# Sliding-window attention and a top-1 mixture of experts: the gate's products on the whole TensorE array, V in two transfers, the first expert's weights split, and a new order

## The chip, the core and the time that is measured

One core of a Trainium2 chip runs the program. The profile calls its engines PE (TensorE; PEld is its weight load), DVE (VectorE), ACT (ScalarE), POOL (GpSimd) and SP (SyncE, which here only issues transfers). The metric is the device time of one execution, in microseconds (us).

## What is computed

Four batches of 768 tokens go through attention with 8 heads of 64. A token attends to the 128 tokens up to itself and to the first four of its batch (the sinks). Each of the 3072 rows of 512 that come out is given to the expert, out of eight, whose gate logit is largest, and is scaled by two gate values.

```python
keep = is_sink | in_window
scores = np.where(keep, scale * np.matmul(q, k.transpose(0, 1, 3, 2)), -1000000000.0)
a = np.exp(scores - np.max(scores, axis=-1, keepdims=True))
x = np.matmul(a / (np.sum(a, axis=-1, keepdims=True) + 1e-09), v)   # then [3072, 512]
logits = x @ w_gate;  e_idx = np.argmax(logits, axis=1)
eom = 1.0 / (1.0 + np.exp(-(x @ w_output_gate)))
for e in range(E):
    mask = e_idx == e
    h = np.maximum(x[mask] @ w1[e], 0.0)          # 512 -> 1024
    out[mask] = gate_w[mask, None] * eom[mask, e, None] * (h @ w2[e])
```

## The kernel before

**Attention.** The work is cut into 16 pairs of heads, four to a batch; `pair(p)` writes one. Its steps on PE are the scores in three groups (L1256, from q and k), six turns of e into f (L1305), the turn of the packed sink weights (`skT`), the products with V in six parts (L1373, `av0` to `av5`), those with the sinks' V (L1396, `avs`), the gate (L1412) and the turns of the output for the store (L1445, `n0`, `n1`). Between them DVE masks the scores and takes the maxima (L1265 to L1272), ACT does the exponentials (L1277) and copies f out (L1308), POOL masks f into g (L384), SP sends the packed sinks to another buffer (L1346), ACT makes a small copy between two parts of `av` (L1387, `tick`) and copies the finished output from PSUM into `ot` (L1402), which the gate and the turns both read. DVE weighs the gate's logits (L1420, `lw`) and scales x (L1448), POOL adds the logits to the batch's (L1428, L1430; DVE in the last two pairs), and SP stores x to `xd` (L1455).

Scores, `av`, `avs` and the gate use 64 x 64 quadrants of the array, four products side by side; everything else uses all 128 x 128. All of attention and the gate is fp32, and each fp32 product shows as two records in the trace. A gate is 24 products with 16 moving columns, 48 records. PE thus changes between two modes, "four" and full; the planner charges 170 ns and 150 ns for a change.

**Routing.** After a batch's last pair, `gate_route` (L524 to L627) turns its logits into positions: DVE steps, one count on PE (L555, L557), then the positions from it (`pos`, `base`, L567, L568), a large compare (`ohrow`, L600), a sort on PE (L619). After batches 1 and 2, `rank_experts` (`u`, L661 and L662) and `early_table` choose two experts each whose tokens so far can be worked on before attention ends: the early slots 0 to 3, 256 tokens each. The other 13 slots (`SEQ`) follow once batch 3 is routed.

**Experts.** A slot gathers its tokens (POOL, L899), turns them (L964), multiplies by w1 (M1), takes relu into hh (ACT), multiplies by w2 (M2), scales (y, L979) and scatters (POOL, L982). Weights arrive as 512 KB transfers into four `raw` buffers. ACT casts each into a high part (L939), DVE subtracts that from raw to make the low part (L943), and a product is then three fp32r products, high by high, low by high, high by low (M1 at L1083, M2 at L1122). With `PLAIN = 1` slot 0 goes another way: its weights land directly in the tiles `wa0` to `wa3`, no casts, and its products are single fp32 ones (M1 at L1064: 32 products of 256 columns; M2 in L1122: 16 of 512). Its M1 may start only behind the last score and its M2 only behind the last pair's `av0`, and both are "soft": the planner puts other ready work of PE ahead of them within a time `SOFT`.

**Order.** No order is written by hand. `Plan.order()` walks all steps with their costs and picks for each engine what is ready and due first; due times are the table `AT` by kind of step, `PIN` by number of step, and `SLOT0` for the experts. Each engine then runs its list in order, so a step that waits holds up all that stand behind it on that engine. `behind=` and `paced` add orders between steps of different engines, `touch` is a small POOL write to a buffer ahead of its first transfer.

## Time and profile before

| | |
|---|---|
| time of three executions | 514.12, 514.47 (median), 519.23 us |
| the profiled execution | 515.66 us; the profile's span in it 514.0 us |
| busy in the span | PE 480.6 us (94%), DVE 326.8 (64%), ACT 281.6 (55%), POOL 159.3 (31%) |
| mean granted clock of PE | 0.99 of full speed |
| moved by DMA | 112.35 MB, 217 GB/s of HBM traffic over the span |
| the first gate starts, the last | 24.50 us, 195.72 us |

Where a row reads `x48`, 48 instructions are meant; `[0.17 <-issue]` at a row's end is idle time ahead of it and what ended it, and "issue" is time in which the engine waited for nothing that the profile shows. The granted clock 1.00 is 2.4 GHz and half of it 1.2 GHz. The chain is the work that ended last, followed back from the end, each step to what released it.

### The profile page before, as it was taken

The page shows a single profiled execution, that of the slowest core. Times are in us where ns is not written, and L with a number is a line of the kernel's source. Part 1 is how long each engine was busy: PE and PEld are TensorE (multiplying, and loading weights), DVE is VectorE, ACT ScalarE, POOL GpSimd, SP SyncE. Part 2 cuts the span into 40 slices and gives each one's busy share as a digit, 9 for nine tenths or more (in the row PEclk, how much of TensorE's full clock was granted, in tenths as well). Part 3 has the DMA queues.
Part 4 walks back from the last instruction along what each step waited for, and adds up shares of the span by engine and source line. Part 5 has one row for each costly group of instructions (what it writes and reads, how often), then busy time and mean ns, then how long its engine had stood idle before and what let it go on. Part 6 is the DMA issues. An engine that isn't in the chain of part 4 may idle for free.

```text
span 514.0 us, 14382 instructions
## 1 busy us (share of the span) xinstructions
PE 480.6 (94%) x5625; PEld 390.4 (76%) x5625; DVE 326.8 (64%) x702; ACT 281.6 (55%) x774; POOL 159.3 (31%) x284
## 2 busy tenths in 40 slices
PE   7899988979899979999999999999999999999993
PEld 3677867757678866688898988978975977986861
DVE  5575866888686667559998963237525688267710
ACT  3878885657597534454556334246525667257510
POOL 5536543647653530204082113022203210101011
PEclk9999999979999999999999999999999999999998
DMA  6674664536695293856498753819679978888930
GB/s 203 214 224 111 220 217 126 169 100 195 200 346 178 87 297 94 282 176 204 153 307 319 233 205 96 294 46 339 199 275 332 331 270 284 301 297 320 352 121 29
DMA packets 61295, 112.35 MB, mean 219 GB/s; under 512 B 8027, under 2 KB 27617, under 8 KB 61218
## 3 DMA queue, kind: packets, MB, share of 16 engines
q1 hardware_dynamic: 56578, 97.06, 56.8%
q0 software_dynamic: 4352, 13.87, 7.5%
q8 instruction: 47, 0.77, 0.6%
q10 hardware_dynamic: 288, 0.41, 0.3%
q14 instruction: 30, 0.25, 0.2%
HBM read 98.14 MB, written 13.31 MB: 217 GB/s over the span
## 4 chain that ended last, share of the span: by engine, by line
PE 62%; DVE 13%; DMA 8%; ACT 6%; issue 6%; POOL 1%; another core or an unknown queue 1%; SPq 1%; POOLq 0%; DVEq 0%; ACTq 0%
PE d L1122 21%; PE d L1083 15%; DMA raw<-in_w_dram 5%; PE d L1373 5%; PE d L1256 4%; PE d L1096 3%; PE d L1064 3%; PE tp L1305 2%; ACT e L1277 2%; DVE nmx L1272 2%; PE tp L964 2%; PE tp L1445 2%; DVE d L1270 2%; PE d L1412 2%; PE d L1030 1%
## 5 line engine op out<-in xcount | busy, mean ns | idle before, releaser
L1277 ACT ACTIVATE e<-d,nmx 128x132 f32<-128x132 f32 x192 | 68.8, 369 | 1.4
L982 POOL DMA_INDIRECT out_dram<-y,idx x20 | 21.2, 1058 | 136.8 <-ACT y L979 107.8
L1000 ACT ACTIVATE hh<-d 128x512 fp32r<-128x512 f32 (+1 forms) x32 | 20.7, 649 | 58.4 <-PE d L1083 56.6
L1256 PE MATMUL d<-k,q 64*64 64x196 f32 (+3 forms) x1088 | 44.2, 283 | 6.8 <-DVE lw L1420 2.0
L1256 PEld LDWEIGHTS d<-k,q 64*64 64x64 f32 x1088 | 36.8, 134 | 15.1 <-issue 6.1
L1003 DVE SCALAR_TENSOR_TENSOR hl<-d,hh 128x512 fp32r<-128x512 f32 (+1 forms) x32 | 24.0, 753 | 34.6 <-ACT hh L1000 34.3
L899 POOL DMA_INDIRECT xg<-xd,idx x20 | 24.5, 1224 | 67.3 <-PE tp L964 44.3
L1373 PE MATMUL d<-f,v 64*64 64x64 f32 (+1 forms) x768 | 41.3, 252 | 2.0 <-ACT e L1277 1.2
L1373 PE MATMUL d<-g,v 64*64 64x128 f32 (+1 forms) x640 | 38.9, 253 | 3.8 <-ACT tick L1387 2.3
L384 POOL TENSOR_SCALAR_AFFINE_SELECT g<-f 128x512 f32<-128x512 f32 (+1 forms) x48 | 27.7, 577 | 43.7 <-ACT f L1308 41.7
L1277 ACT ACTIVATION_READ_ACCUMULATOR e<-d,nmx 128x1 f32 x192 | 39.1, 203 | 0.0
L1373 PEld LDWEIGHTS d<-f,v 64*64 64x64 f32 x768 | 34.1, 135 | 5.9 <-issue 2.5
L1270 DVE COPY_PREDICATED d<-maskf,d 128x512 f32<-128x512 int32 (+1 forms) x48 | 29.0, 604 | 14.0 <-PE d L1256 8.9
L1272 DVE TENSOR_REDUCE nmx<-d 128x4 f32<-128x528 f32 x48 | 33.9, 707 | 1.7
L979 ACT ACTIVATE y<-d,sc 128x512 f32<-128x512 f32 (+1 forms) x28 | 17.5, 656 | 30.6 <-PE d L1122 21.4
L1373 PEld LDWEIGHTS d<-g,v 64*64 64x64 f32 x640 | 29.8, 134 | 5.6 <-ACT tick L1387 3.1
L1305 PE MATMUL tp<-ident,e 128*128 128x128 f32 x192 | 30.3, 285 | 2.4 <-DVE x L1448 1.3
L1308 ACT COPY f<-tp 128x512 f32<-128x512 f32 x48 | 27.5, 586 | 6.6 <-PE tp L1305 6.4
L1305 PEld LDWEIGHTS tp<-ident,e 128*128 128x128 f32 x192 | 21.3, 143 | 10.4 <-DVE x L1448 2.3
L384 POOL TENSOR_SCALAR_AFFINE_SELECT f<-f 128x512 f32<-128x512 f32 (+1 forms) x48 | 27.0, 563 | 3.3
L982 POOL DMA_INDIRECT out_dram<-y,idx_e x8 | 11.8, 1480 | 51.4 <-ACT y L979 49.9
L1284 ACT ACTIVATE nmx<-nmx 128x4 f32<-128x4 f32 x48 | 10.0, 209 | 26.9 <-DVE nmx L1272 26.6
(481 smaller groups left out, 1447.8 us busy)
## 6 DMA issues: line engine op xcount, KB each, us to landing
raw<-in_w_dram SPq DMA_DIRECT2D x96, 512.0 KB
v<-in_vx_dram SPq DMA_DIRECT2D x8, 768.0 KB
xd<-x SPq DMA_DIRECT2D x16, 384.0 KB
k<-in_kx_dram SPq DMA_DIRECT2D x15, 396.0 KB
q<-in_qT_dram SPq DMA_DIRECT2D x15, 384.0 KB
wa1h<-in_w_dram SPq DMA_DIRECT2D x3, 512.0 KB
wa1l<-in_w_dram SPq DMA_DIRECT2D x3, 512.0 KB
wa2h<-in_w_dram SPq DMA_DIRECT2D x3, 512.0 KB
```

The lines of the kernel that those rows point to most:

```text
L384: nc.gpsimd.affine_select(out=ap, in_=ap if src is None else src, pattern=pattern, compare_op=op, fill=fill, base=base, channel_multiplier=cm)
L899: nc.gpsimd.indirect_dma_start(out=p.get(key), out_offset=None, in_=xd[0:n + 1, :], in_offset=bass.IndirectOffsetOnAxis(ap=ids(), axis=0))
L982: nc.gpsimd.indirect_dma_start(out=where, out_offset=bass.IndirectOffsetOnAxis(ap=ids(), axis=0), in_=p.get(yk)[:, 0:m], in_offset=None, b ...
L1083: nc.tensor.matmul(out=p.get(ps)[:, j, 0:cols], lhsT=a, rhs=p.get(x)[:, d, 0:cols], start=d == 0 and i == 0, stop=d == ND - 1 and i == 2)
L1122: nc.tensor.matmul(out=p.get(ys[s][0])[:, ys[s][1], :], lhsT=h[a][:, s * P:(s + 1) * P], rhs=w[b_], start=f == 0 and i == 0, stop=f == NF ...
L1256: nc.tensor.matmul(out=to, lhsT=get(q)[r, qs], rhs=get(k)[r, c:c + n], start=True, stop=True)
L1270: nc.vector.copy_predicated(out=y[:, :, D + 4:3 * D + 4].rearrange("p n (u c) -> p n u c", u=2), mask=bc(maski[:, 1, 4:CW].rearrange("p (u ...
L1272: nc.vector.tensor_reduce(out=top(), in_=z[:, :, :, D:3 * D + 4], axis=AX.X, op=ALU.max, negate=True)
L1277: nc.scalar.activation(out=get(e)[:, t, a, :], in_=by_step()[:, a, i, D:3 * D + 4], func=AF.Exp, bias=get(nmx)[:, a, t:t + 1], scale=SCALE ...
L1305: nc.tensor.transpose(out=get(tp)[:, i, :], in_=get(e)[:, 2 * j + i // 2, i % 2, 4:CW], identity=ident)
L1308: nc.scalar.copy(out=get(f)[:, two].rearrange("p t a r -> p (t a) r"), in_=get(tp))
L1373: nc.tensor.matmul(out=o, lhsT=get(v)[rows_, kt, p % 2 * P + a * D:p % 2 * P + (a + 1) * D], rhs=get((f, g)[src == "g"])[rows_, kt, a, c0: ...
```

## The change

It has four parts.

1. The gate is six products on the full array instead of 24 on quadrants: `lhsT` is a whole 128 x 128 block of `ot`, the moving side is the 32 columns of `wgt` for both heads. The logits lie in PSUM in another arrangement, `gates()`, and `lw` reads them so. The step no longer has the mode "four"; the planner's cost for it stays 700 ns.
2. V of two pairs of heads comes in two transfers of 384 KB, keys 0 to 383 and 384 to 767, each a dependency of its own, so that `av` waits only for the halves that it reads.
3. `PLAIN` is 0. Slot 0's weights go through raw, cast and subtraction like those of the others, and its products are three fp32r ones each. The buffers `hl` and `xl`, which could be opened only after the q, k and e buffers had closed, move to the pool that is open from the start; M1 of slot 0 need not stand behind the last score any more, M2 still stands behind the last pair's `av0`, and neither is "soft".
4. `AT`, `PIN`, `SOFT` and `SLOT0` have new values. A line or two of each table stands in the diff; what they do to the order is shown behind it.

```diff
 NB, RAW = 6, 4
 CW = P + 4
 PAIR, RAT = 9500, 17500
-SOFT = 10509
-SLOT0, STEP, PLAIN, FSTEP = 186561, 20000, 1, 800
+SOFT = 9768
+SLOT0, STEP, PLAIN, FSTEP = 184072, 20000, 0, 800
...
 AT = {
-    "load": -31160, "v": -31097, "vs": -28707, "s0": -1104, "s1": 2946, "s2": 3862, "fold": 6328, "exp": -295,
...
+    "load": -24127, "v": -16807, "vs": -38513, "s0": 687, "s1": 20204, "s2": 9004, "fold": 11988, "exp": -1742,
...
 }
 
 PIN = {
-    9: -2000001, 11: -2000000, 12: -22043, 24: 1242, 25: 1742, 29: 4323, 30: 4823, 54: -67, 55: -2449, 56: -2448,
...
+    7: -2000001, 9: -2000001, 13: -22043, 15: -16806, 16: -16805, 25: 741, 26: 1241, 30: 3820, 31: 3819, 49: 22057,
...
 }
 
 
...
                     continue
                 raw = new(p, "raw", [P, 1024], key=("raw", k, which, i))
                 if k == PLAIN and not which:
-                    touch([raw], lambda raw=raw: p.get(raw), paced[11 + (8 + i) // 3, (8 + i) % 3], at + i)
+                    touch([raw], lambda raw=raw: p.get(raw), paced[11 + (8 * PLAIN + i) // 3, (8 * PLAIN + i) % 3], at + i)
                 key = new(p, "w", None, key=("w", k, which, i))
                 p.inst[key]["make"] = pair_of_weights
 
...
                              ("f", 2, "bp"), ("g", 2, "bp"), ("pk", 2, "bp"), ("hlk", 2, "bp"), ("ot", 2, "bp"), ("tick", 2, "bp"),
                              ("lw", 2, "bp"), ("lg", 2, "bp"), ("nmx", 2, "bp"), ("rs", 4, "bp"),
                              ("w", 0, "a"), ("raw", RAW, "stg"), ("xg", 4, "mx"), ("xh", 1, "mx"), ("sc", 8, "mx"),
-                             ("hh", 4, "m0")):
+                             ("hh", 4, "m0"), ("hl", 4, "m0"), ("xl", 1, "m0")):
             family(fam, n, pool)
         pl.family("w", ["wa%d" % i for i in range(4)], of("a"))
         psks, vsts = [], []
...
             v = ("v", p // 2)
             if p % 2 == 0:
                 new(pl, "v", [P, T, 2 * P], key=v)
-                if p == 2:
-                    touch([v], lambda: get(v)[:, 0, :], paced[0, 1], at)
-                paced["v", p] = pl.op("SP", 2000, lambda: nc.sync.dma_start(out=get(v), in_=vx[b, :, :, hp * P:(hp + 2) * P].rearrange("t p c -> p t c")),
-                      w=[v], at=(at, "v"), size=P * 8 * S, busy=400, behind=[paced["v", p - 2]] if p else ())
+                for i in range(2):
+                    if p:
+                        touch([(v, i)], lambda i=i: get(v)[:, i * T // 2, :], paced[p - 2, 1 + i] if p == 2 else paced[p - 1, 2 * i], at + i)
+
+                    def load_v(i=i):
+                        c = slice(i * T // 2, (i + 1) * T // 2)
+                        nc.sync.dma_start(out=get(v)[:, c], in_=vx[b, c, :, hp * P:(hp + 2) * P].rearrange("t p c -> p t c"))
+                    paced["v", p, i] = pl.op("SP", 2000, load_v, w=[(v, i)], at=(at + i, "v"), size=P * 4 * S, busy=400,
+                                             behind=[paced["v", p - 2, i]] if p else ())
             if p == 0:
                 small_loads()
             if hp == 0:
...
                                              rhs=get((f, g)[src == "g"])[rows_, kt, a, c0:c1], start=i == 0 and kt == 0,
                                              stop=False, skip_group_check=True)
                 ks = sorted(ks, key=str)
+                vr = [(v, x) for x in sorted({kt * 2 // T for kt in kts})]
                 cost = pe(335, "four")
                 if i == 0:
-                    paced["o", p] = pl.op("PE", fn=fn, r=ks + [v], w=[oA, oB], at=(at, "av0"), behind=[paced["o", p - 1]] if p else (), **cost)
+                    paced["o", p] = pl.op("PE", fn=fn, r=ks + vr, w=[oA, oB], at=(at, "av0"), behind=[paced["o", p - 1]] if p else (), **cost)
                     return paced["o", p]
-                return pl.op("PE", fn=fn, r=ks + [v] + [("tick", p)] * (i > 2), w=[("av", p, i)], hold=[o_], behind=begun, at=(at, "av%d" % i), **cost)
+                return pl.op("PE", fn=fn, r=ks + vr + [("tick", p)] * (i > 2), w=[("av", p, i)], hold=[o_], behind=begun, at=(at, "av%d" % i), **cost)
 
             begun = [av(0)]
             for i in range(1, 6):
...
 
             pl.op("ACT", fn=out_copy, r=[oA, oB], w=[(ot, 0), (ot, 1)], at=(at, "ot"), **act(768))
 
+            def gates():
+                return get(o_)[:, :, 3 * P:3 * P + T * 2 * E].rearrange("p u (t a e) -> p u t a e", a=2, e=2 * E)
+
             def gate():
                 for t in range(T):
-                    for h in range(2):
-                        for a, o in enumerate((oA, oB)):
-                            r = slice(a * D, (a + 1) * D)
-                            nc.tensor.matmul(out=bank(o)[h * D:(h + 1) * D, 3, t * 2 * E:(t + 1) * 2 * E], lhsT=get(ot)[r, t, h * D:(h + 1) * D],
-                                             rhs=wgt[r, hp, a * 2 * E:(a + 1) * 2 * E], start=True, stop=True, skip_group_check=True)
-
-            pl.op("PE", fn=gate, r=["wgt", (ot, 0), (ot, 1)], w=[oA, oB], at=(at, "g1"), **pe(700, "four"))
+                    nc.tensor.matmul(out=get(o_)[:, t // 3, 3 * P + t % 3 * 4 * E:3 * P + (t % 3 + 1) * 4 * E], lhsT=get(ot)[:, t, :], rhs=wgt[:, hp, :],
+                                     start=True, stop=True, skip_group_check=True)
+
+            pl.op("PE", fn=gate, r=["wgt", (ot, 0), (ot, 1)], w=[oA, oB], at=(at, "g1"), **pe(700))
             lw = new(pl, "lw", [P, 2, T, 2 * E])
 
             def weigh():
-                lr = get(o_)[:, :, 3 * P:3 * P + T * 2 * E].rearrange("p a (t e) -> p a t e", t=T)
-                tt(out=get(lw), in0=lr, in1=bc(get(rs), 3, 2 * E), op=ALU.mult)
+                tt(out=get(lw).rearrange("p a (u t) e -> p u t a e", u=2), in0=gates(),
+                   in1=bc(get(rs).rearrange("p a (u t) -> p u t a", u=2), 4, 2 * E), op=ALU.mult)
 
             eng, name, cost = (nc.gpsimd, "POOL", {"took": 390, "busy": 410}) if p < NP - 2 else (nc.vector, "DVE", dve(96))
 
...
 
         def close_q():
             qctx.close()
-            opened["mp"] = mctx.enter_context(tc.tile_pool(name="mp", bufs=1, side="right", reuse_waits="tile"))
             opened["b"] = mctx.enter_context(tc.tile_pool(name="wb", bufs=1, side="right", reuse_waits="tile"))
 
         def close_a():
...
 
         xq = pl.op("X", 0, close_q, behind=[i for fam in ("q", "k", "e") for i in on[fam]])
         xa = pl.op("X", 0, close_a, behind=[i for fam in on for i in on[fam]] + [xq])
-        for fam, n, pool, gate, n0 in (("hl", 4, "mp", xq, 0), ("xl", 1, "mp", xq, 0), ("hr", 3, "mc", xa, 0), ("xf", 1, "mc", xa, 0),
+        for fam, n, pool, gate, n0 in (("hr", 3, "mc", xa, 0), ("xf", 1, "mc", xa, 0),
                                        ("xg", 2, "mc", xa, 4), ("y", 4, "mc", xa, 0)):
             family(fam, n, pool, gate, first=n0)
         pl.family("w", ["wb%d" % i for i in range(3)], of("b"), xq)
...
             last = nc.values_load(last_i[0:1, 0:1], min_val=0, max_val=1)
             with tc.If(last > 0):
                 now = tensors(Now())
-                for fam, n, pool, n0 in (("sc", 8, "mx", 0), ("xg", 2, "mc", 4), ("xh", 1, "mx", 0), ("xl", 1, "mp", 0), ("hh", 4, "m0", 0), ("hl", 4, "mp", 0),
+                for fam, n, pool, n0 in (("sc", 8, "mx", 0), ("xg", 2, "mc", 4), ("xh", 1, "mx", 0), ("xl", 1, "m0", 0), ("hh", 4, "m0", 0), ("hl", 4, "m0", 0),
                                          ("hr", 3, "mc", 0), ("y", 4, "mc", 0), ("raw", RAW, "stg", 0)):
                     family(fam, n, pool, p=now, first=n0)
                 now.family("w", ["wa%d" % i for i in range(4)], of("a"))
```

Three places of the order follow. Names such as `q_212` are buffers with a running number; `x24` at a row's end counts instructions that repeat.

**The start of SP's list**, before: the transfers of the first pairs' q and k, of V, of the small tables (`wgt`, `nsw_i`, `xd`) and of the sinks' V (`vst`).

```order
L1207 DMA q_212<-in_qT_dram 128x256
L1217 DMA v_222<-in_vx_dram 128x6x256
L1207 DMA q_212<-in_qT_dram 128x512
L486 DMA wgt<-in_wgo_dram 128x128
L488 DMA nsw_i<-in_nsink_dram 128x2
L488 DMA nsw_i<-in_window_dram 128x2
L489 DMA xd<-tab 128x4
L490 DMA xd<-tab 1x16
L1224 DMA vst_193<-in_vs_dram 8x512 x2
L1207 DMA q_276<-in_qT_dram 128x768
L1207 DMA k_280<-in_kx_dram 128x792
```

And now:

```order
L1220 DMA q_212<-in_qT_dram 128x512
L1220 DMA q_212<-in_qT_dram 128x256
L499 DMA wgt<-in_wgo_dram 128x128
L501 DMA nsw_i<-in_nsink_dram 128x2
L501 DMA nsw_i<-in_window_dram 128x2
L502 DMA xd<-tab 128x4
L503 DMA xd<-tab 1x16
L1234 DMA v_254<-in_vx_dram 128x3x256 x2
L1242 DMA vst_193<-in_vs_dram 8x512 x2
L1220 DMA q_295<-in_qT_dram 128x768
L1220 DMA k_298<-in_kx_dram 128x792
L1242 DMA vst_195<-in_vs_dram 8x512 x2
```

The larger part of q stands first, the small tables stand ahead of V, and V is two transfers. (The first k goes out on ACT's queue in both.)

**DVE's list where the first two batches are counted**, before: `ji` to `ohrow` are the first batch's, `ohb`, `eq` and `z` the second's, `pos` and `base` (formed from the count on PE) the second's too, and L1265 to L1270 begin the masks of a pair.

```order
L590 TENSOR_SCALAR ji<-pi 128x6
L532 TENSOR_TENSOR ohb<-rev_96,tokrev 128x48
L593 CAST jf<-ji 128x12
L594 TENSOR_TENSOR ohj<-jf,ioj 128x96
L538 TENSOR_TENSOR eq<-lg_1443,ohb 128x48
L539 TENSOR_REDUCE z<-eq 128x6
L600 TENSOR_TENSOR ohrow<-io_97,jf 128x768
L567 TENSOR_TENSOR pos<-tp_2103,base 128x48
L568 TENSOR_TENSOR base<-tp_2103,base 128x8
L1265 MEMSET d_120 64x2x4
L1266 COPY_PREDICATED d_120<-maskf,none 128x2x132
L1270 COPY_PREDICATED d_120<-maskf,d_120 128x2x128
```

And now, where the first batch is counted, between `lw` and x of one pair and the masks and the maximum of another:

```order
L1438 TENSOR_TENSOR lw_1356<-d_119,rs_958 128x6x2x16
L1467 TENSOR_TENSOR x_1366<-tp_1351,rs_958 128x512
L1467 TENSOR_TENSOR x_1366<-tp_1361,rs_958 128x256
L580 TENSOR_TENSOR pos<-tp_1391,base 128x48
L581 TENSOR_TENSOR base<-tp_1391,base 128x8
L584 TENSOR_TENSOR pos<-pos,ohb 128x48
L585 TENSOR_REDUCE tokpos<-pos 128x6
L1283 MEMSET d_118 64x2x4
L1284 COPY_PREDICATED d_118<-maskf,none 128x2x132
L1288 COPY_PREDICATED d_118<-maskf,d_118 128x2x128
L1290 TENSOR_REDUCE nmx_1431<-d_118 128x2x2
L601 CAST pi<-tokpos 128x6
```

Before, the two batches' steps are mixed in one stretch: the second batch's `pos` and `base` stand 15 rows behind the first's (rows 153 and 168 of DVE's list, both in the tenth pair). Now the first batch is counted in the seventh pair (row 112) and the second in the eleventh (row 188).

**PE's list around the last gate**, before: for slot 1 `wa0h` is a high part and `wa0l` a low part (for slot 0, `wa2h` and `wa2l` are two transfers of unsplit weights), `xh` and `xl` the tokens' parts, `ot` the pair's output, L1445 its turns.

```order
L1083 MATMUL d_118<-xh_3657,wa0h 128x256
L1083 MATMUL d_118<-xl_3707,wa0h 128x256
L1083 MATMUL d_118<-xh_3657,wa0l 128x256
L1445 MATMUL tp_3765<-ident,ot_3759 128x128 x4
L1445 MATMUL tp_3770<-ident,ot_3759 128x128 x2
L1412 MATMUL d_119<-wgt,ot_3759 64x16 x24
L1122 MATMUL d_120<-wa2h,hh_3453 128x512 x4
L1122 MATMUL d_120<-wa2l,hh_3479 128x512 x4
```

And now:

```order
L1415 MATMUL d_120<-psk_194,vst_195 64x384 x4
L1464 MATMUL tp_3527<-ident,ot_3428 128x128 x2
L1464 MATMUL tp_3536<-ident,ot_3530 128x128 x2
L1464 MATMUL tp_3540<-ident,ot_3530 128x128 x4
L1431 MATMUL d_120<-wgt,ot_3530 128x32 x6
L1135 MATMUL d_119<-wa0h,hh_3288 128x512
L1135 MATMUL d_119<-wa0l,hh_3288 128x512
L1135 MATMUL d_119<-wa0h,hl_3324 128x512
```

Before, 24 products of M1 of slot 1 stand between the last `avs` and the turns that read the last `ot`. Now only two turns of the fifteenth pair's `ot` stand there, and behind the gate come the M2 products of slot 0, in threes. Counted over the whole list, PE's changes of mode up to the last gate fall from 112 to 82.

## Rows read from the trace of the kernel before

**Rows 1.** Page: busy time of each engine, its share, its instructions

```profile
PE 480.6 (94%) x5625; PEld 390.4 (76%) x5625; DVE 326.8 (64%) x702; ACT 281.6 (55%) x774; POOL 159.3 (31%) x284
```

**Rows 2.** Windows between gates' starts: PE PEld DVE ACT POOL busy, PEclk, DMA share, GB/s

```profile
24.50:90.26 65.76, 60.39 (x1618) 49.69 (x1619) 45.07 (x98) 51.77 (x232) 29.78 (x72) 1.00 0.59 183
90.26:102.27 12.01, 10.77 (x253) 8.58 (x252) 10.21 (x32) 8.60 (x37) 7.86 (x16) 1.00 0.57 171
102.27:118.35 16.08, 12.71 (x239) 9.79 (x239) 13.17 (x38) 7.75 (x34) 8.84 (x15) 0.79 0.29 85
118.35:131.64 13.29, 11.92 (x290) 9.76 (x291) 11.50 (x27) 9.82 (x45) 8.29 (x17) 1.00 0.64 197
```

**Rows 3.** The chain in those pairs: start, length, what

```profile
99.36 1.59 DVE ohrow L600
...
103.81 0.97 DVE u L662
...
107.59 1.63 PE d L1256 x20
```

**Rows 4.** Windows, as above: the end of attention, and two stretches of the experts

```profile
143.24:161.01 17.77, 17.47 (x465) 14.68 (x465) 14.41 (x36) 15.24 (x71) 7.89 (x24) 1.00 0.97 314
161.01:195.72 34.71, 31.83 (x439) 27.08 (x438) 20.96 (x57) 16.51 (x42) 15.72 (x24) 1.00 0.49 164
230.00:260.00 30.00, 28.61 (x189) 25.52 (x188) 29.09 (x90) 15.84 (x20) 8.57 (x8) 1.00 0.55 173
380.00:435.00 55.00, 53.30 (x326) 41.30 (x325) 36.84 (x42) 32.91 (x51) 9.95 (x8) 1.00 0.86 296
```

**Rows 5.** Timeline at one gate: start, length, engine, line; [idle before, releaser]

```profile
161.00 0.79 PEld L1412 LDWEIGHTS d<-wgt,ot 64*64 64x64 f32 x48 [0.17 <-issue]
161.01 0.89 PE L1412 MATMUL d<-wgt,ot 64*64 64x16 f32 x48
162.65 0.30 PEld L1064 LDWEIGHTS d<-xh,wa0h 128*128 128x128 f32 x2
164.92 0.23 PEld L557 LDWEIGHTS <-ones 128*128 128x128 bf16 x6
```

**Rows 6.** Instructions by line and form: busy, mean ns | idle before, releasers

```profile
L1412 PEld LDWEIGHTS d<-wgt,ot 64*64 64x64 f32 x768 | 13.1, 134 | 4.9 <-ACT ot L1402 3.3 <-issue 1.6
L1064 PEld LDWEIGHTS d<-xh,wa0h 128*128 128x128 f32 x16 | 2.6, 190 | 0.8 <-issue 0.6
L1402 ACT COPY ot<-d 128x768 f32<-128x768 f32 x16 | 12.8, 798 | 10.5 <-PE d L1396 10.4
L939 ACT CAST wa0h<-raw 128x1024 fp32r<-128x1024 f32 x11 | 11.5, 1048 | 9.6 <-PE d L1096 8.5 <-DMA raw<-in_w_dram 0.6 <-issue 0.3
L943 DVE TENSOR_TENSOR wa0l<-raw,wa0h 128x1024 fp32r<-128x1024 f32 x11 | 13.4, 1218 | 1.9 <-ACT wa0h L939 1.7
L1003 DVE SCALAR_TENSOR_TENSOR hl<-d,hh 128x512 fp32r<-128x512 f32 (+1 forms) x32 | 24.0, 753 | 34.6 <-ACT hh L1000 34.3
```

**Rows 7.** The chain: products of the first experts

```profile
162.92 1.73 PE d L1064 x8
...
203.67 2.88 PE d L1083 x24
...
206.55 6.87 PE d L1122 x16
...
257.61 2.72 PE d L1122 x12
```

**Rows 8.** The chain at the start and in a later expert

```profile
1.74 6.24 DMA q<-in_qT_dram
...
8.40 5.13 DMA k<-in_kx_dram
...
383.90 9.27 DMA raw<-in_w_dram
```

**Rows 9.** Timeline of PE at the first scores

```profile
5.21 0.78 PE L1256 MATMUL d<-k,q 64*64 64x64 f32 x20 [0.60 <-DMA k<-in_kx_dram]
```

More of the change, by code (lines that the diff above doesn't have):

```diff
@@ L51 @@
 PAIR, RAT = 9500, 17500
-SOFT = 10509
-SLOT0, STEP, PLAIN, FSTEP = 186561, 20000, 1, 800
+SOFT = 9768
+SLOT0, STEP, PLAIN, FSTEP = 184072, 20000, 0, 800
 AT = {
-    "load": -31160, "v": -31097, "vs": -28707, "s0": -1104, "s1": 2946, "s2": 3862, "fold": 6328, "exp": -295,
-    "tr0": 5205, "tr1": 8027, "tr2": 9541, "trc": 0, "mask": -3518, "guard": 127, "pack": 3756, "skT": 10500,
[3 rows of a table removed]
+    "load": -24127, "v": -16807, "vs": -38513, "s0": 687, "s1": 20204, "s2": 9004, "fold": 11988, "exp": -1742,
+    "tr0": 2960, "tr1": 8768, "tr2": 12114, "trc": -990, "mask": 6713, "guard": -882, "pack": 3766, "skT": 11336,
[3 rows of a table added]
 }
 PIN = {
[59 rows of a table removed]
[72 rows of a table added]
 }
```

135 rows, old and new, of tables (AT, PIN) are left out of this document.

## The prediction

> **What bounds the kernel now.** I read the page's table of engines first: PE is busy 94% of the span and no other engine over 64% [rows 1]. So a microsecond of work taken from PE, or given to it, should show almost whole, except where PE waits. I then cut attention into windows at the gates' starts. From the first gate (24.50 us) to the eighth (90.26) seven pairs take 65.76 us, 9.39 each, with PE busy 92% of it and DVE 69% [rows 2]. The next three intervals take 12.01, 16.08 and 13.29 us, 41.38 together, 13.2 more than three of 9.39; DVE is busy 34.9 us in them, where three pairs at the earlier rate would need 3 x 45.07 / 7 = 19.3 [rows 2]. That is the routing of batches 0 and 1, which stands there in one stretch of DVE's list. The chain goes through `ohrow` (1.59 us) and `u` (0.97 us) on DVE, so PE stands behind DVE here [rows 3]. PE was busy 12.71 of 16.08 us in the middle interval and its granted clock there is 0.79 [rows 2]: if f of it was at 1.2 GHz and the rest at 2.4, 1 - f/2 = 0.79, so f is 0.42 and 6.8 us ran at half speed. Twenty score records take 1.63 us there [rows 3], 0.78 at the start of the kernel [rows 9].
>
> Behind that, the end of attention has PE busy 17.47 of 17.77 us in two pairs [rows 4], and the early experts are nearly as full: 28.61 of 30 us from 230 to 260, though DVE has 29.09 there and is as full as PE. From 380 to 435 the weight transfers hold DMA at 0.86 [rows 4], and one piece of the chain is a wait of 9.27 us for a raw buffer [rows 8].
>
> **The gate.** 48 weight loads take 0.79 us, the records are 134 ns and the first waits 0.17 us behind the change of mode [rows 5, 6]. They run four at a time on four quadrants: twelve groups, so a group follows the last every (0.79 - 0.13) / 11 = 0.06 us, and a gate costs 0.70 us of PE. Six fp32 products on the full array are twelve loads of 128 x 128. Two such loads take 0.30 us, one 190 ns [rows 5, 6]; the second thus starts 0.11 us behind the first. Twelve are 1.32 us. So I put the change at 16 x (1.32 - 0.70) = **+9.9 us**: fewer instructions, but no longer four side by side. Bounds: if an fp32 load can follow as fast as the six bf16 loads in 0.23 us, 0.04 each [rows 5], a gate is 0.48 us and the change 16 x (0.48 - 0.70) = -3.5. If load and product don't overlap, each record adds its 32 columns: 256 columns are 1.73 / 8 = 0.216 us [rows 7], so 32 are 0.027, a gate is 1.64 us and the change +15.0. I stay at 0.11, the row of the same form and type. The Trainium skill speaks against this edit too: "TensorE: Matmul & The Clock Gate", section "LDWEIGHTS (loading the stationary operand)", says that a load's time goes with its columns and not with its rows, about 107 ns for 128 and 53 for 64. By it a gate would go from 12 x 53 to 12 x 107 ns, an estimate of +10.4 us in all; the rows agree with 0.11 and 0.06.
>
> **Fewer changes of mode.** 30 fewer, 112 to 82. The gate's loads begin 0.17 us late [rows 5]; PE drains the products before it in a part of that, and I take 0.10. That is **-3.0 us**, bounds 0 and -5.1.
>
> **Slot 0 from split weights.** Its M1 was eight pieces of 1.73 us, 13.8, its M2 two of 6.87, 13.7 [rows 7]. A split M1 is four pieces of 24 products in 2.88 us, 11.5, and M2 is 48 products at 2.72 / 12 = 0.227 us, 10.9 [rows 7]. So PE has 22.4 instead of 27.5: **-5.1 us**. In return ACT gets eight casts of 1.05 us and DVE eight subtractions of 1.22 us, 9.8, and up to six smaller ones (four `hl`, two `xl`) of at most 0.75 [rows 6], 14.3 us of DVE work in all. I cost that at nothing, because DVE is busy only 20.96 of 34.71 us in the last two pairs and 14.41 of 17.77 in the two before them [rows 4], 17.1 us free. Without that cover it costs up to 14.3 (rival C).
>
> **Routing spread.** The order counts batch 0 in the seventh pair and batch 1 in the eleventh. A batch's routing is (34.9 - 19.3) / 2 = 7.8 us of DVE. Over two pairs DVE then has 2 x 6.44 + 7.8 = 20.7 us of work where two pairs take 18.8; two batches so cost 3.8 of the 13.2 us, and 9.4 come back. As steps wait for one another as well, I take **-8 us**; of it up to 3.4 us is the half clock (6.8 us at half speed cost at most half of that). Bounds 0 and -13.2. The stretches that now take it up have their own DVE work, so it is the most uncertain term.
>
> **The start.** The first q is in the chain for 6.24 us, and the second pair's k for 5.13 from 8.40 us on [rows 8]. The second part of q stood behind 768 KB of V in SP's list and now stands ahead of it; `av0` can begin with half of V. V is still ahead of the second pair's k, so I take **-1.5 us**, a quarter of the first piece, bounds 0 and -3. Later loads of V were off the chain, so two transfers instead of one (SP's issue and a POOL touch each) I cost at nothing: POOL is busy 31% [rows 1].
>
> **The last two pairs.** The copy into `ot` takes 0.80 us [rows 6]. PE had M1 products of an expert between `avs` and the turns and the gate that read it; now the fifteenth has nothing and the sixteenth two turns of the pair before. **+1.5 us**, twice 0.8; bounds 0 and +2.
>
> **Sum.** +9.9 - 3.0 - 5.1 - 8 - 1.5 + 1.5 = -6.2 us. The profiled execution took 515.7 us, of which the span is 514.0; the median is 514.5, 1.2 below it. The sum goes by durations of one execution and is small, so I put it on the median: 508.3, say **508.5 us**. About 1% (5 us) is what a measurement of this kernel can tell from no change.
>
> **Rivals.**
>
> A, the forecast: PE pays for the gates and gets more back from slot 0, the mode changes and the routing. 503 to 512 us: the routing term between -13 and -5 around the other terms. For it: the 13.2 us of excess with DVE in the chain [rows 2, 3]. Chance 0.52, of which 0.41 are below 509.3 (1% faster).
>
> B, the waits are only moved: DVE's routing makes PE wait as long in two places as it did in one, and the start is bound by the same bytes. 514.5 + 9.9 - 3.0 - 5.1 + 1.5 = 518 us. For it: DVE is at 69% in undisturbed pairs, so the work does not fit into two of them without a rest. Against it: the half clock should go in any case. Chance 0.17, of it 0.04 slower by over 1% (519.6).
>
> C, the other side: the conversions of slots 0 and 1 queue on DVE at the end of attention and make PE wait. Behind the last gate PE has 30 M2 products of slot 0 (6.8 us) before M1 of slot 1 needs its low parts; the point that decides is whether the fourth low part of slot 1 is ready within that. If not, up to DVE's 14.3 us show: 508.5 + 14 = 522 us. For it: DVE is busy 29.09 of 30 us when it converts at full rate [rows 4], and the last two pairs' masks share it. Against it: 17.1 us free before. Chance 0.09, 0.07 of it slower.
>
> D, the gate is cheap: a load that follows another at 0.04 us. The gate then gives -3.5 instead of +9.9: 495 us. For it: six bf16 loads of the same size in 0.23 us [rows 5]. Against it: the fp32 row. Chance 0.08. The same page of the Trainium skill, section "Back-to-back issue gap", sees a floor of about 25 ns for products of up to 64 columns; if that alone counted, twelve would be 0.3 us and the kernel come to an estimated 492; the fp32 loads at 0.11 us disagree.
>
> E, the transfers take part of the gain: PE comes earlier to slots whose weights don't. With DMA at 0.86 from 380 to 435 us [rows 4] and a wait of 9.27 us in the chain [rows 8], I let two thirds of the 6 us be lost: 512.5 us. Against it: transfers start when raw buffers come free, so most of them move along. Chance 0.14.
>
> **Range and chances.** 498 to 518.5 leaves out D below (0.08) and C with the top of B above (about 0.09). The forecast's own range is 503 to 512. Faster by over 1%: 0.41 + 0.08 = 0.49. Slower: 0.04 + 0.07 = 0.11. Within 1%: the rest, 0.11 of A, 0.13 of B, 0.02 of C and 0.14 of E, 0.40.
>
> **What would show it.** Gate: the new line with twelve loads 0.11 us apart and 1.3 us per pair; 0.5 would be D. Routing: the granted clock 1.00 throughout attention, and no interval between gates over 12 us; intervals of 13 us at the seventh and the eleventh pair would be B. Slot 0: M1 in pieces of 2.9 us; low parts of slot 1 ready before PE asks, else C shows as idle PE behind the last gate with a DVE subtraction as what ended it. The start: scores of the second pair earlier than now. The end: if the last gate comes 5 us sooner and the kernel ends only 2 us sooner, it is E. The forecast is wrong by its first term if the gate's products run faster than the fp32 row, and by its fourth if DVE still ends PE's longest waits in attention.

## The result, and the profile after

The changed kernel takes 508.3 us in the median (506.9 to 510.0) where the kernel before took 514.3 in the same job; the ratio is 0.985 with an interval of 0.981 to 0.989, so it is faster by 1.5%, 7.7 us by the ratio and 6.0 by the medians. The forecast was 508.5. The profiled execution took 506.9 us with a span of 505.1, 8.9 less than before. The sum that led to the forecast was nevertheless off in its two largest terms, the gate and the routing, as the experiments and the windows below show; that the number came so close is luck.

The page's table of engines, after (it answers to [rows 1]):

```profile
PE 477.7 (95%) x5097; PEld 401.4 (79%) x5097; DVE 336.1 (67%) x716; ACT 289.0 (57%) x782; POOL 157.5 (31%) x289
```

PE is busy 2.9 us less, DVE 9.3 more. Windows of after, cut at the gates' starts (columns as in [rows 2]): from gate 1 to 7, from 7 to 8, both of these together, and from there to gates 9, 10, 11, 14 and 16:

```profile
23.46:86.94 63.48, 58.80 (x1242) 49.25 (x1240) 45.56 (x105) 47.84 (x216) 32.07 (x77) 1.00 0.50 155
86.94:95.73 8.79, 8.79 (x196) 7.91 (x197) 5.44 (x12) 7.02 (x30) 5.90 (x13) 1.00 0.59 188
23.46:95.73 72.27, 67.59 (x1437) 57.16 (x1436) 51.01 (x116) 54.86 (x245) 37.96 (x90) 1.00 0.51 159
95.73:104.78 9.05, 9.03 (x194) 7.67 (x193) 7.96 (x25) 7.98 (x35) 4.71 (x13) 1.00 0.76 223
104.78:114.64 9.86, 9.10 (x207) 8.08 (x204) 9.42 (x30) 7.13 (x33) 3.54 (x9) 1.00 0.45 132
114.64:128.90 14.26, 12.51 (x237) 10.24 (x235) 11.03 (x24) 12.88 (x55) 10.91 (x27) 1.00 0.85 278
128.90:157.56 28.66, 26.26 (x537) 22.61 (x536) 23.52 (x58) 20.29 (x84) 14.41 (x27) 0.94 0.67 220
157.56:187.64 30.08, 27.87 (x398) 25.13 (x397) 24.93 (x50) 19.46 (x47) 11.64 (x21) 1.00 0.33 106
```

The first gate comes at 23.46 instead of 24.50 us (-1.0). From gate 1 to gate 8 it takes 72.27 instead of 65.76 us (+6.5), from 8 to 11 33.17 instead of 41.38 (-8.2) [rows 2], from 11 to 14 28.66 instead of 29.37 (-0.7), from 14 to 16 30.08 instead of 34.71 (-4.6) [rows 4], and from the last gate to the end 317.46 instead of 318.28 (-0.8). Of the -4.6, some 3 us are only moved: the 24 products of slot 1's M1 that stood ahead of the last gate now stand behind it.

For the first stretch, the kernel before in the same two parts, gates 1 to 7 and 7 to 8:

```profile
24.50:83.59 59.09, 54.17 (x1441) 44.66 (x1444) 40.55 (x88) 47.16 (x210) 27.15 (x65) 1.00 0.58 182
83.59:90.26 6.67, 6.22 (x188) 5.02 (x181) 4.52 (x10) 4.61 (x23) 2.63 (x7) 1.00 0.69 193
```

Timeline of after at the last gate (`tp<-ident,ot` are the turns of the output; start, length, engine, line; idle before):

```profile
186.93 0.87 PE L1464 MATMUL tp<-ident,ot 128*128 128x128 f32 x6 [1.20 <-ACT ot L1421]
187.64 1.42 PE L1431 MATMUL d<-wgt,ot 128*128 128x32 f32 x12
187.53 1.42 PEld L1431 LDWEIGHTS d<-wgt,ot 128*128 128x128 f32 x12
```

Twelve loads in 1.42 us with records of 0.19: one every 0.112 us, as the row for another product of that form had said [rows 5]. PE waits 1.20 us for the copy into `ot`.

The chain of after at slot 0's products (start, length, what; it answers to [rows 7]):

```profile
160.67 2.84 PE d L1096 x24
...
189.06 6.89 PE d L1135 x30
...
198.81 4.12 PE d L1135 x18
```

A piece of M1 takes 2.84 us, M2 6.89 + 4.12 = 11.0. Last, the windows from the last gate to the end give DVE 192.1 us of work before and 196.6 after; the rest, 134.7 of the first 195.7 us before and 139.5 of 187.6 after, lies in attention. So DVE does 4.8 us more there, part 3's subtractions included, and idles 12.9 us less, 48.1 instead of 61.0.

### The profile page after: what moved, and what is told of

Same layout as the page of the kernel before. It is cut to its first block, busy times and chain, and to the rows that moved or that the text cites. A ratio compares the mean times of both kernels' runs of the same rounds, so it can differ in the third digit from the quotient of the medians.

```text
span 505.1 us, 13381 instructions
## 1 busy us (share of the span) xinstructions
PE 477.7 (95%) x5097; PEld 401.4 (79%) x5097; DVE 336.1 (67%) x716; ACT 289.0 (57%) x782; POOL 157.5 (31%) x289
## 4 chain that ended last, share of the span: by engine, by line
PE 48%; issue 17%; DVE 11%; ACT 9%; DMA 9%; POOL 2%; SPq 1%; POOLq 0%; another core or an unknown queue 0%; DVEq 0%; ACTq 0%
PE d L1135 16%; PE d L1096 15%; DMA raw<-in_w_dram 7%; ACT e L1295 4%; PE d L1391 3%; PE d L1274 3%; PE d L1431 3%; PE tp L1323 2%; POOL out_dram L995 2%; DVE nmx L1290 1%; PE tp L1464 1%; PE tp L977 1%; DVE d L1288 1%; DMA k<-in_kx_dram 1%; PE d L1109 1%
## 5 line engine op out<-in xcount | busy, mean ns | idle before, releaser
L1013 ACT ACTIVATE hh<-d 128x512 fp32r<-128x512 f32 (+1 forms) x36 | 23.1, 644 | 49.1 <-PE d L1096 48.9
L912 POOL DMA_INDIRECT xg<-xd,idx x20 | 20.9, 1046 | 83.1 <-PE tp L977 60.3
L1274 PE MATMUL d<-k,q 64*64 64x128 f32 (+3 forms) x1088 | 42.3, 283 | 1.2 <-DMA k<-in_kx_dram 0.6
L1016 DVE SCALAR_TENSOR_TENSOR hl<-d,hh 128x512 fp32r<-128x512 f32 (+1 forms) x36 | 26.7, 745 | 21.1 <-ACT hh L1013 21.0
L1431 PEld LDWEIGHTS d<-wgt,ot 128*128 128x128 f32 x192 | 22.7, 192 | 4.3 <-ACT ot L1421 4.2
L1431 PE MATMUL d<-wgt,ot 128*128 128x32 f32 x192 | 23.5, 273 | 2.3 <-ACT ot L1421 1.8
```

Of the source, the lines that this page charges most:

```text
L1274: nc.tensor.matmul(out=to, lhsT=get(q)[r, qs], rhs=get(k)[r, c:c + n], start=True, stop=True)
L1431: nc.tensor.matmul(out=get(o_)[:, t // 3, 3 * P + t % 3 * 4 * E:3 * P + (t % 3 + 1) * 4 * E], lhsT=get(ot)[:, t, :], rhs=wgt[:, hp, :], st ...
```

## The experiments

Each kernel was timed beside the kernel before on one chip. That kernel took 512.2 to 516.1 us in the median on the chips of the three jobs, so ratios are compared; 0.1% is 0.51 us. Executions of one kernel differ by some 3 us, and the granted clock with them: the four of the changed kernel go from 506.9 us at a mean clock of 0.993 to 510.0 at 0.986. So a single profile serves to find places and not to weigh totals.

| kernel | ratio to before | interval | against the changed kernel |
|---|---|---|---|
| the changed kernel | 0.985 | 0.981 to 0.989 | |
| a_gate24: old gate | 0.980 | 0.975 to 0.985 | -2.5 us |
| a_gate12: gate of twelve | 0.976 | 0.967 to 0.986 | -4.5 us |
| a_act: ACT +10.2 us | 0.986 | 0.981 to 0.991 | +0.4 us |
| a_dve: DVE +11.7 us | 1.002 | 0.999 to 1.005 | +8.7 us |
| a_lo2: slot 0's subtractions twice | 1.002 | 0.999 to 1.005 | +8.8 us |
| a_slot0fp32: slot 0 fp32 on PE | 0.992 | 0.988 to 0.997 | +3.8 us |
| a_exact: part 3 undone | 0.991 | 0.987 to 0.994 | +2.8 us |
| a_exact_gate24: parts 1 and 3 undone | 0.981 | 0.977 to 0.984 | -2.2 us |
| a_v1: part 2 undone | 0.988 | 0.984 to 0.991 | +1.4 us |

| kernel | ratio to before | interval | against the kernel before |
|---|---|---|---|
| b_gate6: new gate in before | 1.000 | 0.996 to 1.004 | -0.2 us |
| b_route_early: batch 0 routed early | 0.999 | 0.995 to 1.003 | -0.6 us |
| b_dve: DVE +12.2 us | 1.009 | 1.006 to 1.012 | +4.6 us |

The last column of the first table is a difference of two ratios times 514 us, uncertain by some 3 us (a_gate12 by 5), that of the second a ratio's distance from 1, uncertain by some 2. The theory at first was the prediction's own: PE bounds attention, so PE's work shows there and DVE's is covered. Its rival: the pace of the pairs is set by a ring of waits through another engine.

**The gate, both ways.** In the changed kernel the old gate, in the same places (`lw` reads the logits in the old arrangement again):

```diff
-                    nc.tensor.matmul(out=get(o_)[:, t // 3, 3 * P + t % 3 * 4 * E:3 * P + (t % 3 + 1) * 4 * E], lhsT=get(ot)[:, t, :], rhs=wgt[:, hp, :],
-                                     start=True, stop=True, skip_group_check=True)
+                    for h in range(2):
+                        for a, o in enumerate((oA, oB)):
+                            r = slice(a * D, (a + 1) * D)
+                            nc.tensor.matmul(out=bank(o)[h * D:(h + 1) * D, 3, t * 2 * E:(t + 1) * 2 * E], lhsT=get(ot)[r, t, h * D:(h + 1) * D],
+                                             rhs=wgt[r, hp, a * 2 * E:(a + 1) * 2 * E], start=True, stop=True, skip_group_check=True)
```

> The changed kernel with the gate alone put back to 24 products on quadrants, in the same places of an order that is otherwise the changed one, word for word. By the sum: 16 gates at 0.70 instead of 1.32 us give -9.9 us, 24 more changes of PE's mode cost +2.4, so -7.5 us against the changed kernel, about 501 us. Rival: PE waits for DVE or ACT behind most gates, so a shorter gate only lengthens those waits: -2 us or less.

And the reverse of it in the kernel before:

> The kernel before with the gate alone made of six products on the full array, in the order of before. By the sum: +9.9 us for the gates, 15 fewer changes of mode -1.5, so +8.4 us, about 522.5 us. Rival: hidden under waits, +2 us or less.

Measured: -2.5 us where -7.5 was expected, and -0.2 where +8.4 was expected. Neither can be told from nothing, and both expected figures lie outside the errors. Windows of a_gate24, from its first gate to its eighth and from its 14th to its last:

```profile
23.59:95.54 71.95, 66.48 (x1688) 55.21 (x1687) 51.07 (x116) 55.26 (x245) 37.95 (x89) 0.98 0.52 160
...
156.25:186.35 30.10, 26.64 (x468) 23.71 (x467) 25.22 (x51) 19.36 (x46) 11.68 (x21) 1.00 0.36 108
```

They take 71.95 and 30.10 us where the changed kernel takes 72.27 and 30.08, with PE busy 1.1 and 1.2 us less: in this execution the shorter gate left PE idle longer. (In the first of them the clock is 0.98, which costs 1.3 us at most.) Windows of b_gate6, from its first gate to its eighth, and from its 14th to its last:

```profile
24.70:90.11 65.41, 63.72 (x1366) 54.04 (x1366) 45.56 (x98) 52.07 (x232) 29.96 (x72) 1.00 0.60 183
...
161.55:199.10 37.55, 34.66 (x368) 29.95 (x367) 20.83 (x57) 16.63 (x42) 15.87 (x24) 0.91 0.46 153
```

Seven pairs take 65.41 us where they took 65.76 [rows 2], with PE busy 63.72 instead of 60.39. The gates' work went into PE's idle time, 5.4 us before and 1.7 now: 0.77 us a pair was free, and 0.62 more was asked by the forecast's figures. (In the last two intervals this execution has a stretch at half clock.)

**A gate of twelve.**

```diff
-                    nc.tensor.matmul(out=get(o_)[:, t // 3, 3 * P + t % 3 * 4 * E:3 * P + (t % 3 + 1) * 4 * E], lhsT=get(ot)[:, t, :], rhs=wgt[:, hp, :],
-                                     start=True, stop=True, skip_group_check=True)
+                    for h in range(2):
+                        nc.tensor.matmul(out=get(o_)[h * D:(h + 1) * D, t // 3, 3 * P + t % 3 * 4 * E:3 * P + (t % 3 + 1) * 4 * E], lhsT=get(ot)[:, t, h * D:(h + 1) * D],
+                                         rhs=wgt[:, hp, :], start=True, stop=True, skip_group_check=True)
```

> The changed kernel with each gate as twelve products of 128 rows by 64 columns, two side by side on the halves of the array, same order. If a load's time goes with its columns and the halves run side by side: twelve groups of two at 0.06 us, 0.7 us a gate, -9.9 us and up to +3.2 for changes into and out of this mode: 498 to 502 us. If the halves don't run side by side: 24 loads at 0.06 are 1.4 us, and the time stays at 508 to 511.

Its first gate in the timeline:

```profile
23.48 0.78 PEld L1432 LDWEIGHTS d<-wgt,ot 128*64 128x64 f32 x24 [0.17 <-issue]
```

24 loads of 128 rows by 64 columns take 0.78 us, as long as 48 of 64 by 64 did [rows 5]: the halves do run side by side, and half the instructions do the same gate. On the time it can't be told from the old gate: -4.5 us, uncertain by 5.

**Which engine sets the pace.** One more step for each pair, on ACT behind the copy into `ot`, or on DVE behind `lw`; nothing else waits for it but what stands behind it on its engine. The third kernel has the DVE step in the kernel before. The tile `extra` is made and set to zero ahead of attention. In `out_copy` of a_act:

```diff
+                nc.scalar.copy(out=extra, in_=extra)
```

In `weigh` of a_dve and b_dve:

```diff
+                tt(out=extra, in0=extra, in1=extra, op=ALU.max)
```

> The changed kernel with one more ACT copy of 512 columns (about 0.57 us) behind the copy into ot of each pair, 9.1 us of ACT work in all; nothing waits for it but ACT itself. If PE's work sets the pace of the pairs: 0 to +1 us, since ACT is busy 57%. If the pace is a ring of waits that goes through ACT, DVE and PE in turn: +4 to +9 us.

> The changed kernel with one more DVE step of 512 columns (about 0.6 us) behind lw of each pair, 9.6 us of DVE work in all; nothing waits for it but DVE itself. If PE's work sets the pace of the pairs: 0 to +2 us. If a ring of waits through DVE sets it: +4 to +10 us.

> The kernel before with one more DVE step of 512 columns behind lw of each pair, 9.6 us of DVE work in all. If DVE sets the pace of the pairs in the kernel before as it does in the changed one: +5 to +9 us. If PE does, as the prediction read it: 0 to +2 us.

The added steps by line and form (busy, mean ns), of a_act, a_dve and b_dve:

```profile
L1425 ACT COPY extra<-extra 128x512 f32<-128x512 f32 x16 | 10.2, 635 | 0.0
```

```profile
L1442 DVE TENSOR_TENSOR extra<-extra 128x512 f32<-128x512 f32 x16 | 11.7, 728 | 0.0
```

```profile
L1423 DVE TENSOR_TENSOR extra<-extra 128x512 f32<-128x512 f32 x16 | 12.2, 763 | 0.0
```

10.2 us of ACT cost 0.4, which is nothing that can be told; 11.7 us of DVE cost 8.7, three quarters of it, in the changed kernel; 12.2 us cost 4.6, 38%, in the kernel before. Against that, 9.9 us of PE less the changes of mode cost 0 in the kernel before and 2.5 in the changed one. So a step of DVE in this place delays the end, a step of ACT does not, and PE's work shows less than DVE's though PE is busier. Where it shows, windows tell: a_dve from its first gate to its eighth, then b_dve from its first to its eighth and from there to its eleventh.

```profile
23.41:101.60 78.19, 71.14 (x1437) 60.18 (x1436) 55.37 (x123) 55.64 (x247) 40.54 (x90) 0.96 0.49 147
```

```profile
24.60:91.52 66.92, 60.55 (x1618) 49.69 (x1619) 49.96 (x105) 51.56 (x232) 32.74 (x72) 1.00 0.59 178
91.52:135.73 44.21, 36.13 (x782) 28.71 (x781) 37.41 (x99) 26.53 (x115) 26.27 (x46) 0.88 0.45 136
```

In the changed kernel seven pairs got 5.9 us longer for 7 x 0.73 = 5.1 us of added DVE steps; a stretch at the lower clock is in it (0.96, which costs 2.8 us at most). In the kernel before the same seven got only 1.2 us longer for 7 x 0.76 = 5.3 us, and the three pairs with the routing 2.8 us for 2.3, again with the lower clock in it (0.88 instead of 0.92 over the three). So in the first seven pairs of the kernel before neither PE nor DVE alone sets the pace: each took most of the added work into its idle time. DVE's work shows more where a routing stands beside the pairs, and in the changed kernel one stands among the first seven; that this is the reason is read from the windows, not shown. Of the 8.7 us a part may come by the clock: its mean is 0.985 in a_dve's ten executions and 0.990 in the changed kernel's four, which by the time lost at half speed is an estimate of 2.6 us at most. The steps were tried in one place of each engine's list only.

**Routing of batch 0 early, alone.**

```diff
+PIN.update({242: 60000, 247: 60001, 248: 60002, 249: 60003, 250: 60004, 251: 60005, 252: 60006, 253: 60007, 254: 60008, 255: 60009, 256: 62000, 257: 62001})
```

> The kernel before with the routing of batch 0 alone given earlier due times, so that it is counted in the seventh pair and not in the tenth with batch 1; the rest of the order shifts a little behind it. By the sum's fourth term: -8 us, about 506 us, and a granted clock of 1.00 in the tenth and eleventh interval. Rival B (waits only moved): within 2 us of before.

Its windows, at gates 1, 8, 9, 10 and 11:

```profile
24.50:91.53 67.03, 63.32 (x1637) 52.54 (x1637) 48.07 (x109) 53.46 (x234) 35.37 (x79) 0.97 0.59 181
91.53:100.21 8.68, 8.53 (x238) 7.45 (x238) 7.00 (x21) 7.51 (x36) 4.67 (x11) 1.00 0.68 214
100.21:119.08 18.87, 14.53 (x289) 10.73 (x289) 15.42 (x42) 12.32 (x55) 9.27 (x15) 0.94 0.45 124
119.08:130.40 11.32, 11.16 (x238) 9.41 (x237) 7.69 (x24) 7.14 (x33) 4.99 (x15) 0.80 0.62 200
```

The count did move to the seventh pair, and the first seven pairs became 1.3 us longer (a clock of 0.97 can account for that). The three intervals behind take 38.87 instead of 41.38 us, but the one from gate 9 to gate 10 still takes 18.87, with batch 1's routing and the ranking in it; the half clock comes some 9 us later and does not go. Over all: -0.6 us, with an interval from -2.5 to +1.4, where -8 was expected. (-8 was the price of both batches; half of it lies outside the interval too.) This is what rival B says, for one batch.

**Slot 0: what PE does, and what covers the conversions.** First the products alone (M2 likewise, on `h[0]` and `w[0]`):

```diff
+                                if k == 0 and p is pl:
+                                    nc.tensor.matmul(out=p.get(ps)[:, j, 0:cols], lhsT=wd.bitcast(F32), rhs=p.get(xh).bitcast(F32)[:, d, 0:cols],
+                                                     start=d == 0, stop=d == ND - 1)
+                                    continue
```

> The changed kernel in its own order, with slot 0's products alone made single fp32 ones on the high parts (M1 32 of 256 columns, M2 16 of 512), PE's work of the kernel before; the conversions stay, the low parts of slot 0 are left out of the products. M1 goes from 11.4 to 13.8 us and M2 from 11.0 to 13.7. If PE's work there is on the path, as the prediction's third term says: +5.1 us, about 513 us. If pairs 14 and 15 have room for M1: +2.7 us from M2 behind the last gate. If neither: 0.

+3.8 us, between the full 5.1 and the 2.7 of M2 alone, and uncertain by 3. Then the subtractions twice:

```diff
-                    tt(out=l, in0=p.get(raw), in1=h.bitcast(F32), op=ALU.subtract)
+                    for _ in range(2 if k == 0 else 1):
+                        tt(out=l, in0=p.get(raw), in1=h.bitcast(F32), op=ALU.subtract)
```

> The changed kernel with each of slot 0's eight subtractions on DVE done twice, 9.8 us of DVE work more. The prediction (their work is covered): within 1 us of the changed kernel. Rival C (DVE late for slot 1): up to +9.8 us, with PE idle behind the last gate until a low part.

+8.8 us of 9.8. The timeline of a_lo2, DVE:

```profile
178.99 2.48 DVE L957 TENSOR_TENSOR wa0l<-raw,wa0h 128x1024 fp32r<-128x1024 f32 x2
...
186.17 2.48 DVE L957 TENSOR_TENSOR wa3l<-raw,wa3h 128x1024 fp32r<-128x1024 f32 x2
188.57 0.68 DVE L1017 SCALAR_TENSOR_TENSOR hl<-d,hh 128x512 fp32r<-128x512 f32 x1
189.17 0.68 DVE L983 TENSOR_TENSOR xl<-tp,xh 128x512 fp32r<-128x512 f32 x1
```

And PE:

```profile
189.91 1.12 PE L1465 MATMUL tp<-ident,ot 128*128 128x128 f32 x4 [5.12 <-DVE xl L983]
```

The four low parts of w2 stand ahead of `hl` and `xl` in DVE's list, and PE's next turns wait for the buffer that `xl` reads: 5.12 us. The window of a_lo2 between its last two gates shows what came of it besides:

```profile
182.10:196.92 14.82, 9.31 (x124) 7.30 (x125) 12.77 (x16) 4.92 (x7) 0.00 (x0) 0.65 0.70 212
```

From 186 to 194 us the granted clock is 0.50, where PE first stands still and then works at half speed. The mean clock is 0.980 in a_lo2's ten executions and 0.990 in the changed kernel's: by the time lost at half speed, an estimate of 5 of the 8.8 us at most. So the 8.8 us hold, beside the wait, a slower clock that came with it.

In the changed kernel itself PE waits only 2.2 us in the last two intervals altogether, 2.1 of it for ACT's copy into `ot` and nothing for DVE, which is idle 5.15 us there. So the eight subtractions are covered, and hardly anything more would be. The next kernel leaves them out, with single fp32 products as in a_slot0fp32 on whole weights, tokens and hidden values:

```diff
+                    nc.scalar.copy(out=h.bitcast(F32) if k == 0 and p is pl else h, in_=p.get(raw))
...
+                    if k == 0 and p is pl:
+                        return
```

> The changed kernel in its own order, with part 3 alone undone: slot 0's weights, tokens and hidden values stay whole fp32 (ACT copies them instead of casting), its products are single fp32 ones, its low parts are left out; DVE loses 8 x 1.22 + 6 x 0.68 = 13.9 us and PE gains the work that slot0fp32 measured at +3.8 us. If every microsecond of DVE there costs 0.9, as the doubled subtractions did: 3.8 - 12.5 = -8.7, about 500 us. If the single subtractions are covered and only the doubled ones were not: PE waits 2.2 us in the two intervals concerned, at most that comes back, 510 to 512 us.

The windows from the 14th gate to the last, of a_exact and of a_slot0fp32, which has the conversions:

```profile
157.12:188.69 31.57, 30.07 (x365) 25.69 (x364) 17.18 (x41) 19.39 (x48) 11.69 (x21) 1.00 0.35 102
```

```profile
157.71:189.29 31.58, 30.08 (x365) 25.70 (x364) 25.46 (x51) 19.47 (x47) 13.42 (x21) 1.00 0.33 102
```

DVE has 25.46 us of work with the conversions and 17.18 without, and the stretch is equally long, with PE equally busy: here the conversions cost nothing. Against the changed kernel PE has 2.2 us more and the stretch is 1.5 us longer. Over all a_exact takes +2.8 us, as for covered conversions. So splitting slot 0 is worth 2.8 to 3.8 us, each uncertain by 3, and its conversions cost nothing that shows. The last of the kind has the old gate as well:

> As a_exact, and the gate of 24 products on quadrants (parts 1 and 3 undone, order and V halves kept). By the gate run before: 2 us or so below a_exact.

It took 503.6 us in the median where a_exact took 507.9 in the same job, -4.3 us, and -5.0 by the ratios, clear of their error of 2.6. Here the gate, with its changes of mode, has a price. PE has more work in these two kernels and DVE less; that PE is thereby closer to being the bound is a reading, since 5.0 and the 2.5 of a_gate24 differ by less than their errors. Last, V in one transfer (a POOL write that starts the second half's buffer now stands behind that transfer, so one column of V is zero in it):

```diff
                     def load_v(i=i):
-                        c = slice(i * T // 2, (i + 1) * T // 2)
+                        if i:
+                            return
+                        c = slice(0, T)
```

> The changed kernel in its own order with part 2 alone undone: V of two pairs comes as one transfer, in the place of the first half, and nothing is sent in the place of the second. The prediction took V's halves for nothing outside the start; the start's -1.5 us came mostly from q. Expected: within 1 us of the changed kernel; the first gate at most 1 us later.

+1.4 us, inside the error of both; its first gate comes at 23.91, 0.45 us later. That the halves matter at the start alone is not contradicted, and not shown.

The kernels with the old gate, or with the gate of twelve, in the new order (0.980, 0.976 and, without the split of slot 0, 0.981) lie below the changed kernel's 0.985, by 2 to 5 us. Their intervals overlap its own, so none is shown to beat it for certain; all three beat the kernel before.

## Why the prediction was right, and where it was not

The time came within 0.2 us of the forecast. Of the steps behind it:

**The bound was misread.** The step "PE is busy 94% and no other engine over 64%, so a microsecond of work given to PE should show almost whole, except where PE waits" failed for the pairs of attention. The share was taken for the bound, and the exception was not applied: [rows 2] had 5.4 us of PE's idle time in seven pairs, more than the 4.3 us that seven gates were to add. For the end of attention it held in part: 2.2 us more of PE's work cost 1.5, but 1.2 us less (the old gates) gave nothing. In the 32.36 us behind the last gate PE is busy throughout, so work taken from it there can show.

**The gate: its size was right, its place was not.** 0.112 us a load, 1.42 us for the whole group, against 0.11 and 1.32. Of the +9.9 us less the changes of mode, 0 showed in the order of before, 2.5 in the new order, which can't be told from 0, and 5.0 where slot 0 was undone as well. Rival D (0.04 us a load) is out. The rule of the Trainium skill (TensorE: Matmul & The Clock Gate, section "LDWEIGHTS (loading the stationary operand)") that a load goes with its columns also agrees with the gate of twelve: 128 rows by 64 columns take no longer than 64 by 64.

**The changes of mode** (-3.0) were not tried by themselves. The old gate brought 24 of them back (106 in its trace up to the last gate, 82 in the changed kernel's), so the price measured for the gate is the gate's less theirs, and the forecast for the two together was 7.5.

**Slot 0** (-5.1): the pieces came as worked out, 2.84 and 11.0 us for 2.88 and 10.9, and 2.8 to 3.8 us of it reach the end. That DVE covers the conversions was right with little to spare. Rival C's mechanism appeared only under the doubled subtractions, and at another point: not slot 1's fourth low part behind the gate, but w2's four in front of the last pair's turns.

**Routing** (-8) is the other term that failed, as far as one profile of each kernel tells. The three intervals gave back 8.2 us as forecast, at a clock of 1.00. But the first seven pairs became 6.5 us longer. 4.0 of that lies between gates 4 and 7 (32.78 us instead of 28.75), where batch 0's routing now stands, from 61.5 to 80.6 us on DVE; 2.1 lies between gates 7 and 8, where 44 more records of other products of PE have moved in (196, against 188 less 36 for the gate). So a batch took up to 4 us from these pairs, the gates' price included, and not 1.9: its 7.8 us were spread over two pairs' idle time of DVE, as if that could be filled. Gate 1 to gate 11 is 1.7 us shorter in all (+6.5 - 8.2); with ten gates' share of a price of 2.5 to 5.0 the routing gave 3 to 5 us there. The signs named for it failed too: three intervals between gates are over 12 us (12.87, 12.24 and 14.26), and the half clock did not go but came as 0.94 in the stretch from 128.90 to 157.56 us, where the forecast looked for 1.00 throughout.

**The start** (-1.5): -1.0. The second pair's scores start at 13.59 us instead of 13.66; only the first pair gained. **The last two pairs** (+1.5): PE waits 0.93 and 1.20 us for `ot` at the last two gates, and in the kernel before at neither, so +2.1, a little over the bound of 2. The last copy into `ot` began only at 186.08 us, behind a cast of slot 1's weights on ACT (185.13, 1.05 us).

**Rival E**, a gain lost to transfers, is out: the last gate comes 8.1 us sooner in the profiled execution and the end 8.9.

**Why the sum still came out.** By the runs the gate with its 24 changes of mode costs 2.5 to 5.0 us where the sum had 9.9 - 2.4 = 7.5, so it was priced 2.5 to 5 us too dear. Slot 0 gives 2.8 to 3.8 where the sum had 5.1, some 1.3 to 2.3 too much. What is left of the -7.7, some -6 to -10 us, falls to the new order and V's halves (these -1.4 at most), for which the sum had -8.6 with the routing as its main term. Each of these figures is uncertain by some 3 us, so they show that errors of opposite sign met, and not that they cancel to 0.2 us: that is luck. The order was not run by itself, as the numbers of the steps differ between the kernels and a table doesn't carry over, and routing early alone gave nothing that can be told. That DVE idles 12.9 us less up to the last gate is seen in the profile; how much of it is the order's doing, and which of its rows, stays open.

## What to carry to other kernels

A busy share says how much room an engine has, not who sets the pace: in seven pairs of the kernel before, PE at 92% took 3.3 us more work for nothing, and DVE at 69% took 4.9 us more for 1.2 us; in the changed kernel, where a routing stands among these pairs, 11.7 us of small steps on DVE cost 8.7 over the whole. Before pricing work on the busiest engine, set it against that engine's idle time in the same stretch; and to find what sets the pace, add a small step that nothing waits for, on one engine after the other, and see in which stretch the time grows. When work moves to a less loaded stretch, charge it there at the rate that such a step shows, not at zero. And look at the mean granted clock of all executions: in a_lo2 the stretch at half clock behind PE's wait cost time beside the wait itself.

## What the runs showed of the hardware

DVE's small steps were slow beside POOL's expansions (`rhs`). Timeline of after in the ranking behind batch 1 (the first line) and in the routing of batch 2, DVE and POOL:

```profile
112.09 0.22 DVE L685 TENSOR_TENSOR pe<-perm,io 128x16 f32<-128x16 f32 x1
...
170.92 0.17 DVE L684 TENSOR_TENSOR perm<-rank,io 128x16 f32<-128x16 f32 x1
171.12 1.05 DVE L685 TENSOR_TENSOR pe<-perm,io 128x16 f32<-128x16 f32 x1
...
172.96 1.01 DVE L693 COPY had<-taken 128x8 f32<-128x8 f32 x1
...
176.10 0.15 DVE L688 TENSOR_REDUCE od<-pe 128x2 f32<-128x16 f32 x1
```

```profile
171.09 3.86 POOL L621 TENSOR_TENSOR rhs<-oh,ohj 128x512 bf16<-128x512 bf16 x3 [1.14 <-DVE perm L684]
```

The same instruction of 16 columns (L685) took 0.22 us at 112.09, where POOL's next expansion began at 112.92, and 1.05 us at 171.12 beside the first of three. The copy of 8 columns (L693) took 1.01 us beside them; in the kernel before it stood clear of the expansions and took 0.37. The expansion at 112.92 took 1.04 us on POOL, so the long steps are about as long as one expansion. The Trainium skill (GPSIMD Engine Reference, section "1. Specifications") says that the two engines share interfaces to SBUF and contend for steps of DVE with two SBUF inputs or in a two-port mode; the trace agrees for the first kind of step (`pe` has two inputs), and in which mode the copy ran it does not show. No run here takes POOL's steps away. It would make a routing's cost on DVE depend on what POOL does meanwhile.
